# Pooled attention and a PReLU feed-forward on one core: PReLU from PSUM in the first chunk only, the first loads in runs, and a new order of the first phase

## The chip, the cores and the metric

The kernel runs on one core of one Trainium2 chip. A core has five engines that work side by side: TensorE (PE in the profile, with its weight loads as PEld), VectorE (DVE), ScalarE (ACT), GpSimd (POOL) and SyncE (SP), which here only issues DMAs. Each engine works through its own list of instructions in order and waits at semaphores for the others. PE writes into PSUM, a small memory of banks that DVE and ACT read; everything else lies in SBUF. The metric is the device time of one execution in microseconds (us); lower is better.

## The reference

```python
def _attn_ref(q, k, v):                      # each 8 x 8 x 576 x 64, f32
    k_p = k.reshape(B, H, Sp, pool, D).mean(axis=3)      # pool = 8, Sp = 72
    v_p = v.reshape(B, H, Sp, pool, D).mean(axis=3)
    scores = scale * np.matmul(q, k_p.transpose(0, 1, 3, 2))
    scores = scores - np.max(scores, axis=-1, keepdims=True)
    attn = np.exp(scores)
    attn = attn / (np.sum(attn, axis=-1, keepdims=True) + 1e-09)
    return np.matmul(attn, v_p)

def _moe_ref(x, w_in, w_out, alpha):         # x: 4608 x 512, the attention's output
    h = x @ w_in                             # w_in: 512 x 2048
    g = np.maximum(h, 0.0) + alpha * np.minimum(h, 0.0)
    return g @ w_out                         # w_out: 2048 x 512
```

The two weight matrices arrive as 64-bit floats, the rest as 32-bit ones.

## The kernel before

The 4608 tokens are worked on in 9 chunks of 512. PE multiplies 16-bit floats only, so every operand is scaled by a power of two and split into a high and a low half, and each product is three matmuls (low x high, high x low, high x high).

**One chunk.** Attention: k and v are pooled over 8 rows, q and k are split, `scores` (L598 to L600) makes the 128 x 576 scores of one of the four tiles of a chunk, and the softmax takes one of two paths. On the DVE path, DVE takes the maximum (L511), subtracts it (L525), ACT takes the exponential (L528), DVE sums (L530). On the ACT path, ACT does exponential and sum at once, head by head, in eight pairs of instructions (L521). Then the quotient (L536, POOL or DVE), the split into high half (ACT, L541, twice: the high half is needed at two places of the padded tile) and low half (POOL, L544 and L547), a transposing DMA (L552) and `mix` (L609), attention times v. ACT and DVE turn that into x (L566, L570). Feed-forward: for each of 16 slices f of 128 hidden units, "F1(f)" is twelve matmuls into one PSUM bank h (L766 to L768). ACT reads h and scales it to t in SBUF (`ffn1_scaled`, L772); DVE computes the larger of h x `ra` and t (`ffn1_prelu`, L776), reading h from PSUM; ACT rounds the result to the high half of g (L784), POOL subtracts for the low half (L787). F1(f) uses one of two h banks in turn, so F1(f+2) can start only when all readers of F1(f)'s bank are done. "F2" is 192 matmuls (L813 to L815) that sum g times the second weights into o; ACT scales o (L803) and SP stores it (L808).

**Two parts of the program.** The first phase (`start`) does the attention and feed-forward of chunk 0, loads and converts all weights, and does the attention of chunk 1. Its order is written by a planner (`_Plan`): each operation has an engine, an assumed duration, and a rank; the table `RK` holds the numbers that set the ranks and choose engines. The planner sets the order of every engine's list; the waits follow from what is read and written. A weight tile (two slices f) goes through: maximum over the high words (L242), scale factors, ACT on the low words (L647), ACT on the high words (L653 for the first weights, L657 for the second), two DVE operations that join the words (L660, L663), and for the first weights the high half on ACT (L683) and the low half on POOL (L702), for the second weights high on ACT (L688), low on DVE (L691). In chunk 0, FFN2 runs slice by slice over four banks, so its step f needs the second weights of slice f. `reduce_max` spreads a maximum over all partitions by ACT (L206), PE (L209) and DVE (L212, L217, then L233 and L238 for scale factors).

The other part is the loop over chunks 1 to 8: F1 and F2 of chunk c with the attention of chunk c+1 between them. Tile's scheduler sets its order. SP takes its list in order there too: the transposes of a chunk, then the k, q and v loads of the next but one, output stores, v loads.

Of the kernel before, what the change touches and what calls it, by code (L numbers as in the profile page):

```python
# [13 lines left out]
ALU = mybir.AluOpType  # L14
# [6 lines left out]
SP = S // POOL  # L21
# [3 lines left out]
P = 128  # L25
# [30 lines left out]
def _new_b(c):  # L56
# [2 lines left out]

RK = dict(k_pool=1, ps1=6, ps2=8, s_pool=0, w2_dve=16, lo_dve=0, l1=405.5, step=2.27, l2=548.61, mx1=198.3,
          mx1s=-26.1, mx2=186.66, mx2s=49.92, grp=52.93, grps=11.45, cv1=100.17, cv1s=47.71, r2=-639.49,
          cv2=443.89, cv2s=136.71, low1=145.54, low2=-143.62, lo1=644.52, lo2=79.0, sc=128.8, pre=-280.21,
          hi=98.27, lo=349.48, step2=33.01, a1=-147.09, al=314.3, td=99.45, ld1=42.46, ld2=-86.65, q0=186.92,
          v0=69.06, sm0=38.36, sms0=24.77, mix0=351.57, q1=94.05, v1=145.47, sm1=23.77, sms1=-49.07,
          mix1=-28.53)


ROOM = dict(d=3, big=12, f=4, e=3, v=3)  # L70
# [66 lines left out]
def pooled_attention_prelu_ffn(ctx: ExitStack, tc: tile.TileContext, qT, kT, vT, kN, vN, w1, w2, alpha, out):  # L137
# [56 lines left out]
    def reduce_max(add, r, m, n, *after, narrow=False, cap=None, rank=0.0):  # L194

        ps = once(lambda: ps_s.tile([P, 2, CH], F32, tag="s", name="pm"))
        t = once(lambda: sml.tile([P, n], F32, tag="pt", name="pt", bufs=2))

        def spread(j, dg):
            nc.scalar.activation(dg(), ident, AF.Copy, scale=m()[:, j:j + 1])  # L206
# [13 lines left out]
        xs_ = []  # L220
        for j in range(n):
            dg = once(lambda: sml.tile([P, P], BF16, tag="pd", name="pd", bufs=ROOM["d"]))
            x = add("ACT", 0.28, lambda j=j, dg=dg: spread(j, dg), *after, rank=rank, take="d")
            xs_.append(add("PE", 0.15, lambda j=j, dg=dg: bring(j, dg), x, rank=rank, take=None if j else "S", give="d"))
        return add("DVE", 0.4 + 0.13 * n, lambda: (maxima(), clamp()), *xs_, rank=rank, give="S")

# [26 lines left out]
    def load(add, dst, src, us, rank, *after, **kw):  # L253
        return add("SP", us, lambda: nc.sync.dma_start(out=dst(), in_=src), *after, rank=rank, **kw)  # L254
# [11 lines left out]
    def pooled(add, src, dst, rank, by_rows, behind=()):  # L266

        t = big_tile([P, 4, DM], "nat")  # L270
        u = once(lambda: fp.tile([P, DM], F32, tag="f", name="nat4"))
        ps = once(lambda: ps_s.tile([P, 2, CH], F32, tag="s", name="pl"))
        lds = []
        for j in range(2):
            lds += 2 * [load(add, lambda j=j: t()[:, 2 * j:2 * j + 2],
                             src[2 * j * P:(2 * j + 2) * P].rearrange("(a p) n -> p a n", p=P), 1.6, rank,
                             *behind, *lds[-1:], take=None if j else "big")]
        lds.append(load(add, lambda: u()[:S - 4 * P], src[4 * P:], 0.4, rank, lds[-1], take="f"))

        def products(j):  # L280
            rows, n = (t()[:, j], P) if j < 4 else (u(), S - 4 * P)
            win = pool[:n, w0 - P // POOL * j:w0 - P // POOL * j + SP]
# [18 lines left out]
    def big_tile(shape, name):  # L301
        return once(lambda: big.tile(shape, F32, tag="big", name=name))

    def attention(add, c, bs, rank, begin=False, early=False, k_pool=0, q_cuts=1, on_act=(), on_dve=(), behind=()):

# [27 lines left out]
        ql = []  # L333
        qt = big_tile([P, 2, NPR, HC], "qraw")
        for i in range(2):
            dst, dep = lambda i=i: qt()[:, i], [*behind, *[x[1] for x in ql]]
            if early and i == 0:
                dst, dep = lambda: kq()[:, NPR * S:].rearrange("p (a t) -> p a t", a=NPR), [kl[bs[0]][0][3]]
            ql.append((dst, load(add, dst, qT[c, i], 1.46, rank + 1, *dep, take="big" if i == early else None)))
# [159 lines left out]
        for i in range(TPC):  # L499
# [9 lines left out]
            def top(i=i, mx=mx, sv=sv):  # L509
                descale(c, i)  # L510
                nc.vector.tensor_reduce(out=mx(), in_=sv(), axis=AX.X, op=ALU.max)  # L511
            x = add("DVE", 0.8, top, x, rank=rk)
            nb = once(lambda: sml.tile([P, 2, 4], F32, tag="nb", name="nb", bufs=4))
            if i in on_act:
                x = add("DVE", 0.2, lambda i=i, nb=nb, mx=mx: nc.vector.tensor_scalar(
# [2 lines left out]
                for q in range(4):  # L518
                    def exps(i=i, ex=ex, nb=nb, sm=sm, sv=sv, b=q // 2, q=q % 2):
                        for h in (2 * q, 2 * q + 1):  # L520
                            nc.scalar.activation(ex()[:, b, h], sv()[:, b, h], AF.Exp, scale=descale(c, i),  # L521
                                                 bias=nb()[:, b, h:h + 1], accum_out=sm()[:, b, h:h + 1])
                    x = add("ACT", 0.8, exps, x, rank=rk, take=None if q else "e", give="S" if q == 3 else None)
            else:
                x = add("DVE", 0.73, lambda ex=ex, mx=mx, sv=sv: nc.vector.tensor_tensor(  # L525
                    out=ex(), in0=sv(), in1=mx().broadcast_to([P, 2, 4, SP]), op=ALU.subtract),
# [11 lines left out]
            ev_ = lambda ex=ex: ex().rearrange("p b h s -> p (b h) s")  # L538
            y = []
            for l in range(2):  # L540
                x = add("ACT", 0.67, lambda l=l, ap=ap, ev_=ev_: nc.scalar.copy(out=ap[:, l, :, :SP], in_=ev_()),  # L541
                        x, *td[i - 2:i - 1], rank=rk)
                y.append(x)
# [86 lines left out]
    def max_w(l, i):  # L630
        absmax((m1, m2)[l - 1][:, 2 * i:2 * i + 2], word(l, i, 1))

    def picked(f, n, of=NF):

        return (f + 1) * n // of > f * n // of

    def convert(add, l, i, begin, sc, rank):
# [8 lines left out]
        if wide:  # L646
            low = add("ACT", 1.15, lambda: nc.scalar.activation(  # L647
                word(l, i, 0).bitcast(I32), word(l, i, 0).bitcast(U32), AF.Copy, scale=LOW3), w_ld[l, i],
                      rank=rank + RK[f"low{l}"])
        if l == 1:  # L650
            x = begin
            for j in range(2):
                x = add("ACT", 0.66, lambda j=j: nc.scalar.activation(  # L653
                    u()[:, j], word(l, i, 1)[:, j], AF.Copy, scale=y1[:, 2 * i + j:2 * i + j + 1]),
                    begin, x, rank=rank, take=None if j else kind)
# [116 lines left out]
        nc.scalar.activation(t, hps[c, f], AF.Copy, scale=rp[:, f:f + 1])  # L772

    def ffn1_prelu(c, f):
        t = hs[c, f]
        nc.vector.scalar_tensor_tensor(out=t, in0=hps.pop((c, f)), scalar=ra[:, f:f + 1], in1=t,  # L776
                                       op0=ALU.mult, op1=ALU.max)

    def ffn1_parts(c, f, l):
# [46 lines left out]
    def start():  # L826
# [68 lines left out]
    class _Line:  # L895
# [5 lines left out]
        def add(self, engine, us, emit, *after, **kw):  # L901
            self.ops.append(emit)
# [59 lines left out]
```

## Time and profile before

| what | value |
|---|---|
| three runs | 907.07, 900.93, 902.24 us |
| median | 902.24 us |
| the profiled execution | 903.4 us, of which its span is 901.7 us |
| DVE, ACT, POOL busy | 407.2, 430.6, 347.8 us |
| bytes moved | HBM read 45.10 MB, written 9.44 MB |

The profile is of one execution. Its span is the time from the first to the last instruction; 1.7 us of the execution lie outside it. A row of the timeline has the start, the duration, the engine, the line, the tile written and those read, and in brackets how long the engine stood idle before it and what ended that. The table by stretches has, for each stretch, the busy time of each engine and PEclk, the share of full speed that TensorE's clock was granted. Times of the tables count from the start of the span.

### The profile page before, as it was taken

Reading aid. Unit: us, or ns where it says so; the run is one execution under the profiler, and the core shown is the slowest. Engines: PE = TensorE matmul, PEld = TensorE weight load, DVE = VectorE, ACT = ScalarE, POOL = GpSimd, SP = SyncE. Lnnn points to the kernel's source line nnn. Section 1 sums busy time; section 2 is a strip of 40 time slices with the busy share of each in tenths; the row PEclk is TensorE's granted clock in tenths of the full one; section 3 lists DMA queues with packets and bytes.
Section 4 is the critical chain, followed back from the end, with each engine's and each line's share of the span. In section 5 each row is a group of like instructions: output and inputs, shape, how many; then the busy total and the mean of one; then the engine's idle time right before and its main releaser. Section 6 shows DMA issues by size and latency. Waiting matters only on the chain.

```text
span 901.7 us, 11443 instructions
## 1 busy us (share of the span) xinstructions
PE 846.9 (94%) x4404; PEld 405.8 (45%) x4404; DVE 407.2 (45%) x657; ACT 430.6 (48%) x727; POOL 347.8 (39%) x375
## 2 busy tenths in 40 slices
PE   5779899989898989999989999999989999999998
PEld 4444354444344444454435444544444444444443
DVE  4889895484128520762077116621572145111110
ACT  5899984555324631563246234632464346313330
POOL 1357364376214730564055504640455027302320
PEclk9889999999999999999999999999999999999999
DMA  9686033606210360045012601260115004000000
GB/s 331 218 264 257 25 86 65 198 4 156 87 51 4 71 172 24 27 74 172 24 27 51 172 36 39 48 175 36 39 27 117 36 13 77 18 35 12 1 23 25
DMA packets 93638, 74.73 MB, mean 83 GB/s; under 512 B 77040, under 2 KB 77616, under 8 KB 93584
## 3 DMA queue, kind: packets, MB, share of 16 engines
q1 hardware_dynamic: 93584, 74.01, 29.2%
q8 instruction: 34, 0.56, 0.3%
q14 instruction: 20, 0.16, 0.1%
HBM read 45.10 MB, written 9.44 MB: 60 GB/s over the span
## 4 chain that ended last, share of the span: by engine, by line
PE 65%; DVE 11%; issue 7%; ACT 6%; DMA 6%; POOL 4%; SPq 1%; POOLq 0%; DVEq 0%; ACTq 0%
PE o L813 10%; PE o L814 10%; PE o L815 10%; PE h L766 9%; PE h L767 9%; PE h L768 9%; DMA vraw<-vT_dram 3%; POOL g L787 3%; DVE t L776 2%; DVE e L233 2%; DVE q L446 1%; PE x L609 1%; DMA nat<-kN_dram 1%; SPq L254 1%; ACT q L442 1%
## 5 line engine op out<-in xcount | busy, mean ns | idle before, releaser
L787 POOL TENSOR_TENSOR g<-t,g 128x512 f16<-128x512 f32 x144 | 166.9, 1160 | 397.7 <-ACT g L784 393.4
L776 DVE SCALAR_TENSOR_TENSOR t<-h,m,t 128x512 f32<-128x512 f32 x144 | 107.0, 744 | 308.4 <-ACT t L772 303.7
L766 PE MATMUL h<-x,w 128*128 128x512 f16 x576 | 220.0, 384 | 17.2 <-DVE t L776 13.9
L767 PE MATMUL h<-x,w 128*128 128x512 f16 x576 | 221.2, 384 | 0.0
L768 PE MATMUL h<-x,w 128*128 128x512 f16 x576 | 221.1, 384 | 0.0
L813 PE MATMUL o<-w,g 128*128 128x512 f16 x544 | 206.1, 380 | 10.7 <-POOL g L787 10.5
L814 PE MATMUL o<-w,g 128*128 128x512 f16 x544 | 206.4, 379 | 0.0
L815 PE MATMUL o<-w,g 128*128 128x512 f16 x544 | 204.4, 380 | 0.0
L772 ACT ACTIVATE t<-h,rp 128x512 f32<-128x512 f32 x144 | 97.5, 682 | 117.4 <-PE h L768 96.2
L784 ACT CAST g<-t 128x512 f16<-128x512 f32 x144 | 88.6, 615 | 99.0 <-DVE t L776 98.3
L803 ACT ACTIVATE o<-o,os 128x512 f32<-128x512 f32 x34 | 23.1, 687 | 156.3 <-PE o L815 156.3
L767 PEld LDWEIGHTS <-w 128*128 128x128 f16 x576 | 56.9, 99 | 83.4 <-issue 23.9
L813 PEld LDWEIGHTS <-g 128*128 128x128 f16 x576 | 56.3, 98 | 79.7 <-POOL g L787 13.1
L768 PEld LDWEIGHTS <-w 128*128 128x128 f16 x576 | 57.0, 99 | 69.7 <-issue 3.5
L815 PEld LDWEIGHTS <-g 128*128 128x128 f16 x576 | 56.4, 98 | 67.8 <-issue 0.3
L766 PEld LDWEIGHTS <-w 128*128 128x128 f16 x576 | 56.5, 99 | 65.9 <-issue 4.0
L814 PEld LDWEIGHTS <-g 128*128 128x128 f16 x576 | 56.4, 98 | 65.0 <-issue 0.6
L467 POOL TENSOR_TENSOR vraw<-vraw 72x512 f32<-72x512 f32 (+1 forms) x56 | 53.7, 972 | 43.0 <-DMA vraw<-vT_dram 39.2
L570 DVE SCALAR_TENSOR_TENSOR x<-x,xsc,x 128x512 f16<-128x512 f32 x36 | 26.1, 748 | 65.5 <-ACT x L566 65.5
L536 POOL TENSOR_TENSOR e<-e,sm 128x576 f32<-128x576 f32 x35 | 40.5, 1158 | 34.6 <-DVE sm L534 33.6
L541 ACT CAST apad<-e 128x576 f16<-128x576 f32 x72 | 44.9, 669 | 14.6 <-POOL e L536 12.4
L544 POOL TENSOR_TENSOR apad<-e,apad 128x448 f16<-128x448 f32 x36 | 37.3, 1035 | 17.7 <-ACT apad L541 17.6
(135 smaller groups left out, 840.6 us busy)
## 6 DMA issues: line engine op xcount, KB each, us to landing
w<-w_dram SPq DMA_DIRECT2D x16, 1024.0 KB
out_dram<-o SPq DMA_DIRECT2D x36, 256.0 KB
qraw<-qT_dram SPq DMA_DIRECT2D x17, 512.0 KB
vraw<-vT_dram SPq DMA_DIRECT2D x28, 288.0 KB
kraw<-kT_dram SPq DMA_DIRECT2D x12, 576.0 KB
kq<-kT_dram SPq DMA_DIRECT2D x2, 576.0 KB
nat<-kN_dram SPq DMA_DIRECT2D x2, 512.0 KB
nat<-vN_dram SPq DMA_DIRECT2D x2, 512.0 KB
```

Source lines behind the costliest of these rows:

```text
L467: nc.gpsimd.tensor_tensor(out=o, in0=y, in1=z, op=ALU.add)
L541: x = add("ACT", 0.67, lambda l=l, ap=ap, ev_=ev_: nc.scalar.copy(out=ap[:, l, :, :SP], in_=ev_()), x, *td[i - 2:i - 1], rank=rk)
L766: nc.tensor.matmul(ps, w[:, 1, ks_], x[:, 0], start=(n == 0), stop=False)
L767: nc.tensor.matmul(ps, w[:, 0, ks_], x[:, 1], start=False, stop=False)
L768: nc.tensor.matmul(ps, w[:, 0, ks_], x[:, 0], start=False, stop=(n == NK - 1))
L772: nc.scalar.activation(t, hps[c, f], AF.Copy, scale=rp[:, f:f + 1])
L776: nc.vector.scalar_tensor_tensor(out=t, in0=hps.pop((c, f)), scalar=ra[:, f:f + 1], in1=t, op0=ALU.mult, op1=ALU.max)
L784: nc.scalar.copy(out=g[:, 0], in_=t)
L787: nc.gpsimd.tensor_tensor(out=g[:, 1], in0=t, in1=g[:, 0], op=ALU.subtract)
L813: nc.tensor.matmul(ps, g[:, 1, ts_], w[:, 0], start=(f == 0), stop=False)
L814: nc.tensor.matmul(ps, g[:, 0, ts_], w[:, 1], start=False, stop=False)
L815: nc.tensor.matmul(ps, g[:, 0, ts_], w[:, 0], start=False, stop=(f == NF - 1))
```

## The change

Four things are changed.

1. `ffn1_prelu`: in chunks 1 to 8 DVE reads t instead of h, with `al` instead of `ra` (t is h times `rp`, and `ra` is `rp` times `al`, so it is the same quantity). Both inputs then lie in SBUF, and ACT is the only reader of the h bank. Chunk 0 is as before.
2. `pooled` and `attention`: the two halves of k (and of v) for chunk 0 are issued one behind the other as one operation of the planner; the q halves no longer count as dependent on each other.
3. The softmax paths are chosen by bits of `RK`: in chunk 0 only tile 2 takes the ACT path (tiles 0 and 2 before), in chunk 1 only tile 1 (tiles 0 and 1 before). The quotient of tile 0 goes from DVE to POOL. For tiles 0, 1 and 3 of chunk 0 the second copy of the high half is a DMA within SBUF instead of ACT.
4. A new table `RK` and some new assumed durations: a new order of the first phase. One of eight first-weight tiles has its low half on DVE instead of POOL, one of 16 second-weight slices on ACT and POOL instead of DVE, and one of eight second-weight tiles is joined in SBUF instead of PSUM.

Cut to its core:

```diff
-RK = dict(k_pool=1, ps1=6, ps2=8, s_pool=0, w2_dve=16, lo_dve=0, l1=405.5, step=2.27, l2=548.61, ...
+RK = dict(oa0=4, od0=0, oa1=2, ad0=11, ad1=0, v_pool=0, k_pool=1, ps1=6, ps2=7, s_pool=0, w2_dve=15, lo_dve=1,
...
-            lds += 2 * [load(add, lambda j=j: t()[:, 2 * j:2 * j + 2],
-                             src[2 * j * P:(2 * j + 2) * P].rearrange("(a p) n -> p a n", p=P), 1.6, rank,
-                             *behind, *lds[-1:], take=None if j else "big")]
+        def halves():
+            for j in range(2):
+                nc.sync.dma_start(out=t()[:, 2 * j:2 * j + 2],
+                                  in_=src[2 * j * P:(2 * j + 2) * P].rearrange("(a p) n -> p a n", p=P))
+        lds = 4 * [add("SP", 3.2, halves, *behind, rank=rank, take="big")]
...
+                if l and i in by_dma:
+                    y.append(add("SP", 0.5, lambda ap=ap: nc.sync.dma_start(out=ap[:, 1, :, :SP], in_=ap[:, 0, :, :SP]),
+                                 x, rank=rk))
+                    continue
...
     def ffn1_prelu(c, f):
-        t = hs[c, f]
-        nc.vector.scalar_tensor_tensor(out=t, in0=hps.pop((c, f)), scalar=ra[:, f:f + 1], in1=t,
+        t, h = hs[c, f], hps.pop((c, f))
+        nc.vector.scalar_tensor_tensor(out=t, in0=t if c else h, scalar=(al if c else ra)[:, f:f + 1], in1=t,
                                        op0=ALU.mult, op1=ALU.max)
...
-        xd, td = attention(add, 0, [0], 0.0, begin=True, q_cuts=2, on_act=(0, 2), on_dve=(0,))
+        xd, td = attention(add, 0, [0], 0.0, begin=True, q_cuts=2, on_act=bits("oa0"),
+                           on_dve=bits("od0"), by_dma=bits("ad0"))
```

Three places of the order. First SP's list from the start: `nat` is k or v of chunk 0 (by its `kN` or `vN` source), `qraw` is q, `al` is alpha, `w` a weight tile. Before:

```order
L254 DMA nat<-kN_dram 128x2x512
L254 DMA qraw<-qT_dram 128x1024
L254 DMA al<-al_dram 128x16
L254 DMA w_134<-w_dram 128x2x1024
L254 DMA nat<-kN_dram 128x2x512
L254 DMA qraw<-qT_dram 128x1024
L254 DMA w_175<-w_dram 128x2x1024
L254 DMA nat_193<-kN_dram 64x512
```

Now:

```order
L276 DMA nat<-kN_dram 128x2x512 x2
L254 DMA nat_132<-kN_dram 64x512
L254 DMA qraw<-qT_dram 128x1024 x2
L254 DMA al<-al_dram 128x16
L254 DMA w_163<-w_dram 128x2x1024
L254 DMA w_180<-w_dram 128x2x1024
L276 DMA nat<-vN_dram 128x2x512 x2
L254 DMA nat_243<-vN_dram 64x512
```

All of k, then all of q, stand ahead of the first weight tile, and v stands behind the second weight tile instead of behind the eighth.

Second, DVE's list in the first phase around the last PReLUs of chunk 0 (`t`): `w_605` and `w_681` are the first second-weight slices (L691, now L705, is their low half), `kbd` and `q` the low halves of chunk 1's k and q. Before:

```order
L429 SCALAR_TENSOR_TENSOR kbd_95<-ks,s,kbd_95 64x4x72
L691 SCALAR_TENSOR_TENSOR w_605<-v,s_124,w_605 128x512
L429 SCALAR_TENSOR_TENSOR kbd_95<-ks,s,kbd_95 64x4x72
L446 SCALAR_TENSOR_TENSOR q_982<-kq,s,q_982 128x1024
L663 SCALAR_TENSOR_TENSOR v<-w_703,vw 128x1024
L776 SCALAR_TENSOR_TENSOR t<-h,m_122,t 128x512 x2
L585 TENSOR_SCALAR ds<-e 128x1
```

Now:

```order
L790 SCALAR_TENSOR_TENSOR t<-h,m_122,t 128x512
L432 SCALAR_TENSOR_TENSOR kbd_95<-ks,s,kbd_95 64x4x72
L705 SCALAR_TENSOR_TENSOR w_681<-v,s_124,w_681 128x512
L432 SCALAR_TENSOR_TENSOR kbd_95<-ks,s,kbd_95 64x4x72
L449 SCALAR_TENSOR_TENSOR q_1032<-kq,s,q_1032 128x1024
L705 SCALAR_TENSOR_TENSOR w_681<-v,s_124,w_681 128x512
L677 SCALAR_TENSOR_TENSOR v<-w_754,vw 128x1024
```

The low halves of k, q and of the first second-weight slices have moved from ahead of the last PReLU to behind it.

Third, PE's list behind the mix for chunk 2 (the row with `aT` and `v16`), with the semaphores it waits for. Before:

```order
L609 MATMUL x_2263<-aT_1908,v16_1836 64x384
L766 LDWEIGHTS w1_134 [waits DVE_49]
L766 MATMUL h_2390<-x16_2257,w1_134 128x512 [waits Activation_49]
L766 LDWEIGHTS w1_134
L766 MATMUL h_2422<-x16_2257,w1_134 128x512 [waits DVE_49]
L813 LDWEIGHTS g_2128 [waits Pool_49]
L813 MATMUL o_2131<-w2_784,g_2128 128x512
```

Now, and (the last row) further down at the third F1 of that chunk:

```order
L616 MATMUL x_2289<-aT_1934,v16_1862 64x384
L827 LDWEIGHTS g_1669
L827 MATMUL o_2312<-w2_681,g_1669 128x512
```

```order
L780 MATMUL h_2482<-x16_2283,w1_163 128x512 [waits Activation_49]
```

Before, two products of the next chunk's F1 and an F2 product that reads the chunk's last slice of g stand directly behind the mix; now F2 of the chunk's third tile, with the oldest slice of g, stands there. An F1 that takes over an h bank waited for DVE and now waits for ACT.

More of the change, by code (lines that the diff above doesn't have):

```diff
@@ L58, in _new_b @@
     return [b for _, _, b in _segs(c) if b > prev]
[L62 to L67, printed above, removed]
+RK = dict(oa0=4, od0=0, oa1=2, ad0=11, ad1=0, v_pool=0, k_pool=1, ps1=6, ps2=7, s_pool=0, w2_dve=15, lo_dve=1,
+          l1=451.63, step=2.76, l2=439.38, mx1=223.95, mx1s=-38.27, mx2=267.52, mx2s=50.59, grp=66.84,
+          grps=8.65, cv1=-42.31, cv1s=60.37, r2=-403.82, cv2=826.06, cv2s=147.64, low1=83.05, low2=-213.14,
+          lo1=717.27, lo2=97.15, sc=136.57, pre=-255.44, hi=44.61, lo=345.22, step2=29.56, a1=-20.76,
+          al=308.29, td=-23.43, ld1=94.39, ld2=42.23, q0=321.84, v0=94.52, sm0=-105.72, sms0=0.87, mix0=310.16,
+          q1=66.1, v1=144.72, sm1=133.56, sms1=-54.48, mix1=58.45)
 ROOM = dict(d=3, big=12, f=4, e=3, v=3)
@@ L222, in reduce_max @@
             dg = once(lambda: sml.tile([P, P], BF16, tag="pd", name="pd", bufs=ROOM["d"]))
-            x = add("ACT", 0.28, lambda j=j, dg=dg: spread(j, dg), *after, rank=rank, take="d")
+            x = add("ACT", 0.39, lambda j=j, dg=dg: spread(j, dg), *after, rank=rank, take="d")
             xs_.append(add("PE", 0.15, lambda j=j, dg=dg: bring(j, dg), x, rank=rank, take=None if j else "S", give="d"))
@@ L272, in pooled @@
         ps = once(lambda: ps_s.tile([P, 2, CH], F32, tag="s", name="pl"))
-        lds = []
-        for j in range(2):
-            lds += 2 * [load(add, lambda j=j: t()[:, 2 * j:2 * j + 2],
-                             src[2 * j * P:(2 * j + 2) * P].rearrange("(a p) n -> p a n", p=P), 1.6, rank,
-                             *behind, *lds[-1:], take=None if j else "big")]
-        lds.append(load(add, lambda: u()[:S - 4 * P], src[4 * P:], 0.4, rank, lds[-1], take="f"))
+        def halves():
[3 more added lines that the diff above has]
+        lds = 4 * [add("SP", 3.2, halves, *behind, rank=rank, take="big")]
+        lds.append(load(add, lambda: u()[:S - 4 * P], src[4 * P:], 0.4, rank, take="f"))
         def products(j):
@@ L302, in big_tile, with attention @@
         return once(lambda: big.tile(shape, F32, tag="big", name=name))
-    def attention(add, c, bs, rank, begin=False, early=False, k_pool=0, q_cuts=1, on_act=(), on_dve=(), behind=()):
+    def attention(add, c, bs, rank, begin=False, early=False, k_pool=0, q_cuts=1, on_act=(), on_dve=(), by_dma=(),
+                  behind=()):
         n = len(bs) + 2
@@ L335, in attention @@
         for i in range(2):
-            dst, dep = lambda i=i: qt()[:, i], [*behind, *[x[1] for x in ql]]
+            dst, dep = lambda i=i: qt()[:, i], [*behind, *([] if begin else [x[1] for x in ql])]
             if early and i == 0:
@@ L511, in top @@
                 nc.vector.tensor_reduce(out=mx(), in_=sv(), axis=AX.X, op=ALU.max)
-            x = add("DVE", 0.8, top, x, rank=rk)
+            x = add("DVE", 0.95, top, x, rank=rk)
             nb = once(lambda: sml.tile([P, 2, 4], F32, tag="nb", name="nb", bufs=4))
@@ L522, in exps @@
                                                  bias=nb()[:, b, h:h + 1], accum_out=sm()[:, b, h:h + 1])
-                    x = add("ACT", 0.8, exps, x, rank=rk, take=None if q else "e", give="S" if q == 3 else None)
+                    x = add("ACT", 1.25, exps, x, rank=rk, take=None if q else "e", give="S" if q == 3 else None)
             else:
@@ L631, in max_w, with bits @@
         absmax((m1, m2)[l - 1][:, 2 * i:2 * i + 2], word(l, i, 1))
+    def bits(name):
+        return [i for i in range(TPC) if RK[name] >> i & 1]
     def picked(f, n, of=NF):
@@ L649, in convert @@
                       rank=rank + RK[f"low{l}"])
-        if l == 1:
+        if l == 1 and picked(i, RK["v_pool"], NF // 2):
+            x = add("Pool", 2.3, lambda: nc.gpsimd.tensor_tensor(
+                out=u(), in0=word(l, i, 1), in1=y1[:, 2 * i:2 * i + 2].broadcast_to([P, 2, 512]), op=ALU.mult),
+                begin, rank=rank, take=kind)
+        elif l == 1:
             x = begin
             for j in range(2):
-                x = add("ACT", 0.66, lambda j=j: nc.scalar.activation(
+                x = add("ACT", 0.72, lambda j=j: nc.scalar.activation(
                     u()[:, j], word(l, i, 1)[:, j], AF.Copy, scale=y1[:, 2 * i + j:2 * i + j + 1]),
@@ L887, in start @@
             x = [add("PE", 2.59, lambda f=f: step(f), gd[f], wd[2, f], *x, rank=due[2](f))]
-        attention(add, 1, [1], L2 + RK["a1"], early=True, k_pool=int(RK["k_pool"]), on_act=(0, 1), behind=[ld[2, NF // 2 - 1]])
+        attention(add, 1, [1], L2 + RK["a1"], early=True, k_pool=int(RK["k_pool"]), on_act=bits("oa1"),
+                  by_dma=bits("ad1"), behind=[ld[2, NF // 2 - 1]])
         for i in (2, 3, 0, 1):
```

## The prediction

> **What bounds the kernel now.** I read the page, the table by stretches, PE's waits, then the timeline where PE stood. The page:
>
> ```profile
> PE 846.9 (94%) x4404; PEld 405.8 (45%) x4404; DVE 407.2 (45%) x657; ACT 430.6 (48%) x727; POOL 347.8 (39%) x375
> ```
>
> PE is busy for 94% of the span of 901.7 us. What can be won without touching PE's own work is its 54.8 us of idle time and what a slow clock costs. Whose they are is told by cutting the span at the first F1 matmul (62.03), the end of chunk 0's F1 (111.6) and the first F1 of chunk 1 (161.7). The columns are length, then busy time of PE, PEld, DVE, ACT, POOL, then PEclk, DMA share and GB/s:
>
> ```profile
> 0.00:62.03 62.03, 40.88 (x246) 28.42 (x246) 42.94 (x95) 47.27 (x101) 20.24 (x34) 0.91 0.80 257
> 62.03:111.60 49.57, 45.87 (x198) 19.60 (x196) 46.84 (x65) 46.01 (x68) 29.97 (x24) 0.94 0.45 176
> 111.60:161.70 50.10, 47.48 (x285) 23.44 (x286) 38.51 (x61) 32.38 (x73) 25.32 (x31) 1.00 0.34 68
> 161.70:901.69 739.99, 712.63 (x3678) 334.35 (x3677) 278.95 (x438) 304.94 (x489) 272.23 (x287) 0.99 0.24 63
> ```
>
> Four stretches, four limits. The opening is ACT's and the loads'. In F1 of chunk 0 DVE (46.84) and ACT (46.01) are both full. F2 of chunk 0 is PE's. In chunks 1 to 8 PE is busy for 712.63 of 739.99, and 27.4 us are idle. PE's two long waits there (us in total, times, longest):
>
> ```profile
> PE h L766 <- DVE t L776: 12.9, 7, 2.6
> PE o L813 <- POOL g L787: 10.5, 6, 3.4
> ```
>
> So 12.9 us go to F1 waiting for DVE's PReLU to give the h bank back, and 10.5 us to F2 waiting for the low half of g. Two of these waits in the timeline; the first is in chunk 2:
>
> ```profile
> 273.46 1.15 POOL L787 TENSOR_TENSOR g<-t,g 128x512 f16<-128x512 f32 x1
> 273.53 2.79 DVE L233 TENSOR_SCALAR e<-pr 128x3 int32<-128x3 int32 x1
> 274.57 0.61 POOL L467 TENSOR_TENSOR vraw<-vraw 72x256 f32<-72x256 f32 x1
> 275.14 1.15 POOL L787 TENSOR_TENSOR g<-t,g 128x512 f16<-128x512 f32 x1
> 276.73 1.09 ACT L426 ACTIVATE kbd<-ks,s 64x288 f16<-64x288 f32 x2 [2.47 <-DVE s L238]
> 277.30 1.36 DVE L429 SCALAR_TENSOR_TENSOR kbd<-ks,s,kbd 64x288 f16<-64x288 f32 x2
> 277.85 2.19 ACT L442 ACTIVATE q<-qraw,s 128x1024 f16<-128x1024 f32 x2
> 279.03 2.48 DVE L446 SCALAR_TENSOR_TENSOR q<-qraw,s,q 128x1024 f16<-128x1024 f32 x2 [0.37 <-ACT q L442]
> 279.94 1.24 ACT L772 ACTIVATE t<-h,rp 128x512 f32<-128x512 f32 x2
> 281.43 0.75 DVE L776 SCALAR_TENSOR_TENSOR t<-h,m,t 128x512 f32<-128x512 f32 x1
> ...
> 282.23 0.38 PE L766 MATMUL h<-x,w 128*128 128x512 f16 x1 [2.32 <-DVE t L776]
> 282.44 0.38 PE L767 MATMUL h<-x,w 128*128 128x512 f16 x1
> ```
>
> A DVE instruction on three numbers takes 2.79 us, ending as three POOL instructions in a row end (276.29). ACT's k and q work waits behind it, ACT reaches t at 279.94, DVE the PReLU at 281.43, and PE starts at 282.23. Matmuls follow each other at 0.215 us. The second wait is at the seam of two chunks:
>
> ```profile
> 230.76 3.06 POOL L467 TENSOR_TENSOR vraw<-vraw 72x512 f32<-72x512 f32 x3 [7.03 <-DMA vraw<-vT_dram]
> 233.78 1.15 POOL L787 TENSOR_TENSOR g<-t,g 128x512 f16<-128x512 f32 x1
> 234.99 0.39 PE L813 MATMUL o<-w,g 128*128 128x512 f16 x1 [3.43 <-POOL g L787]
> ```
>
> POOL sat at v instructions whose load was late; g stood behind them and PE behind g.
>
> **The change, chunks 1 to 8.** The PReLU keeps its count and its size; read from SBUF I give it the 0.74 us it has now:
>
> ```profile
> L776 DVE SCALAR_TENSOR_TENSOR t<-h,m,t 128x512 f32<-128x512 f32 x144 | 107.0, 744 | 308.4 <-ACT t L772 303.7
> L691 DVE SCALAR_TENSOR_TENSOR w<-v,s,w 128x512 f16<-128x512 f32 x16 | 13.5, 880 | 0.0
> L784 ACT CAST g<-t 128x512 f16<-128x512 f32 x144 | 88.6, 615 | 99.0 <-DVE t L776 98.3
> ```
>
> L691 is the same operation with both inputs in SBUF and takes 0.88. What changes is who frees the bank: the order shows PE waiting for ACT. At 282 that would have been about 280.6 (first t of the pair at 279.94, 0.69 long) instead of 282.2, so 1.5 of that 2.3 us. The new PE order does more. Counted from the built order at 0.215 us a matmul, between the last F1 product of a slice and the first F2 that reads its g there were 3.8 to 5.3 us of other PE work at the start of chunks 1 to 8, now 7.9 in chunks 2 to 8 (5.6 in chunk 1); between F1(0) and F1(2) 1.2 to 2.7, now 2.7 (0.4 in chunk 1). A slice needs t, PReLU and high half (0.68 + 0.74 + 0.62) and POOL's 1.16, 3.2 us in all with no queue, so 7.9 leaves room for the 3.4 us wait above. And the seam is gone: half of the mixes no longer have an F2 on the newest g behind them.
>
> Against it stands that DVE's 128 PReLUs now may meet POOL. Here is one that did, in the opening:
>
> ```profile
> 26.29 0.73 DVE L446 SCALAR_TENSOR_TENSOR q<-qraw,s,q 128x512 f16<-128x512 f32 x1
> 27.13 2.46 POOL L702 TENSOR_TENSOR w<-v,w 128x1024 f16<-128x1024 f32 x1 [8.94 <-ACT w L683]
> 27.61 2.52 DVE L446 SCALAR_TENSOR_TENSOR q<-qraw,s,q 128x512 f16<-128x512 f32 x1
> ```
>
> The same operation takes 0.73, and 2.52 when it comes while POOL works: it ends 0.54 us after POOL does. The Trainium skill says so in general ("SBUF — State Buffer", section "Who interferes with whom"): a DVE instruction with two SBUF inputs contends with a GpSimd instruction that reads SBUF, and whoever comes second is blocked for the other's whole length. The trace agrees, with 2.52 against 0.73. POOL is busy for 272.23 of 740 us, and one g takes 1.16, so a PReLU that arrives at random waits 0.37 x 0.58 = 0.2 us, and 1.16 behind a full one. Both are less than the new room, so I count the price as nothing on the path; its upper bound is the first rival.
>
> So of 27.4 us idle I keep 8 (chunk 1's short distances, the k and q work on ACT, which still holds t) and take back 2 of the some 7 us that PEclk 0.99 costs: 712.6 - 2 + 8 = 719, that is -21. Bounds: no idle and full clock 707; nothing won 740.
>
> **The opening.** The chain of waits there runs along ACT for most of its last 18 us. The rows that price this part and the next (the first from the chain, the second from stretches of 36 us, the third again from the chain):
>
> ```profile
> 32.94 3.26 ACT e L521 x16
> 0.00:36.00 36.00, 21.89 (x142) 18.26 (x142) 22.67 (x53) 23.36 (x48) 6.65 (x16) 0.98 0.90 329
> 198.09 1.75 DMA v<-v
> L528 ACT ACTIVATE e<-e,ds 128x576 f32<-128x576 f32 x32 | 24.8, 774 | 10.6 <-DVE e L525 10.3
> L541 ACT CAST apad<-e 128x576 f16<-128x576 f32 x72 | 44.9, 669 | 14.6 <-POOL e L536 12.4
> L647 ACT ACTIVATE w<-w 128x1024 int32<-128x1024 uint32 x16 | 18.1, 1149 | 2.8 <-DMA w<-w_dram 2.8
> L653 ACT ACTIVATE vw<-w,y 128x512 f32<-128x512 f32 x12 | 8.7, 722 | 0.6 <-DVE x L570 0.5
> L683 ACT CAST w<-v 128x1024 f16<-128x1024 f32 x8 | 8.3, 1036 | 0.1
> L663 DVE SCALAR_TENSOR_TENSOR v<-w,vw 128x1024 int32<-128x1024 int32 x14 | 17.1, 1219 | 0.0
> 113.64 1.40 DVE L776 SCALAR_TENSOR_TENSOR t<-h,m,t 128x512 f32<-128x512 f32 x2
> 145.60 2.28 DVE L691 SCALAR_TENSOR_TENSOR w<-v,s,w 128x512 f16<-128x512 f32 x3
> ```
>
> Ahead of its first t, ACT has eight exponential pairs fewer (3.26 us), three copies (2.0), two L653 (1.4) and one L683 (1.0), and one more L528 (0.8): -6.9 us. But DVE now sets a bound. The loads are the same 11.8 MB (36 us at 329 GB/s), so the last weight tile still lands at about 35; k and v only come sooner. After the maximum of that tile, DVE has, counted from the order at the rows' durations, about 18 us of work until the first x: 35 + 18 + 3 for waits = 56, and F1 at 57 instead of 62. That is -5; bounds 0 (DVE's waits are 8) and -6.9. No row shows the copies by DMA that replace ACT's; the nearest, a copy of v within SBUF, takes 1.75 us, and tile 3's stands straight ahead of the last transpose: 1.75 for 0.67, which the 3 us hold. If they cost nothing that way, ACT is the bound and F1 starts at 55.1.
>
> **F1 of chunk 0.** Between first and last t, ACT loses two q (2.2), two k (1.1) and two low words (2.3), and gains two L653 (1.4), one L683 (1.0) and a high half (0.6): -2.6. DVE loses four L691 (3.5), one q (1.2) and two k (1.4), and gains two operations as long as a join (2.4): -3.7. Both full engines shrink, ACT less, so 49.6 becomes 47.0; bounds 41.3 (192 matmuls) and 49.6.
>
> **F2 of chunk 0.** What left F1 arrives here: three L691 (2.6), a q (1.2), two k (1.4), one more join (1.2), and subtraction and sum of a tile on the DVE path (some 1.5), so DVE's 38.5 becomes 46.4 of 50.1. PE covers that only while each second-weight slice is ready for its FFN2 step. Before, the last L691 ended at 147.88, 32.8 us after the last PReLU at 115.04, with 26.7 us of work by the order, 1.23 times as long. The new order puts slice 13 at 32.5 us of work, x 1.23 = 40; PReLU ends some 2 us after F1, so 42 after F1's end, where PE comes at 37.5. So a wait of some 4.5 us against the 2.6 idle now: 52.0, +1.9. Bounds 47.5 and 57.
>
> **Sum** against the profiled execution: 57 + 47 + 52 + 719 = 875 span, +1.7 outside = 876.7 against 903.4. The median lies 1.2 lower, so 875.5.
>
> **Rivals.**
> - *Lock-out.* POOL's instructions follow each other without a gap, and the row at 273.53 shows DVE losing three times running. In the interleaved part a slice takes PE 18 x 0.215 = 3.9 us, and ACT's list alternates t and high half, so t of the next slice waits for the PReLU: 0.68 + 0.74 + 0.62 = 2.0. It decides from a mean wait of 1.9 us per PReLU. At two full g (2.3) each of 13 slices in 8 chunks loses 0.4: +42, with the old idle time kept and 7 won before: 937. Against it: POOL's g needs the PReLU itself, so POOL runs dry. 6%. If whoever comes second is always blocked, as that page has it, this is where it shows.
> - *The idle time stays.* ACT's k and q work (3.3 us from 276.73) still stands ahead of t, and the 2.79 us wait still comes. Then 719 is 738: 894. 16%.
> - *The first phase gives nothing.* DVE sets the start and then FFN2: 62 + 49.6 + 55 + 719: 886. 18%.
> - *The bank isn't freed sooner.* The order's wait on ACT excludes it; with what else could fail, 4% at 902.
>
> **How the numbers follow.** The forecast has 56% and its own range 864 to 886. The range of 8 in 10 takes in the third rival and nearly the second: 861 to 893. A measurement of this kernel can tell about 1% (9 us) from no change: faster 0.83, same 0.11, slower 0.06.
>
> **What would show it.** F1 starts at 55 to 59. In chunks 1 to 8 "PE h <- DVE t" is gone and "PE o <- POOL g" is under 4 us; PE's idle time there is 3 to 14. L790 has a mean between 0.75 and 1.1; over 2.5 is the first rival. Chunk 0's FFN2 shows PE waiting for DVE's second-weight halves. I am wrong if PE waits for ACT t by more than 12 us in the chunks, or if F1 starts after 60.

## The result and the profile after

The changed kernel takes 878.12 us (median of 874.56, 877.46, 878.79 and 878.85) against 902.62 us: a ratio of 0.971, with an interval of 0.967 to 0.976. The forecast was 875.5. The sum is nearly right, but its parts are not. The profiled execution has a span of 877.1 us; the page's line of engines, and the stretches cut at the same places as before (first F1, end of chunk 0's F1, first F1 of chunk 1):

```profile
PE 840.6 (96%) x4445; PEld 406.5 (46%) x4445; DVE 429.4 (49%) x658; ACT 422.8 (48%) x695; POOL 371.1 (42%) x376
```

```profile
0.00:66.95 66.95, 45.36 (x286) 31.05 (x287) 40.35 (x92) 40.16 (x79) 19.31 (x34) 0.80 0.76 228
66.95:115.50 48.55, 43.46 (x199) 18.95 (x198) 47.48 (x60) 45.14 (x68) 32.44 (x25) 1.00 0.52 203
115.50:165.09 49.59, 48.03 (x285) 23.50 (x283) 39.97 (x65) 33.67 (x60) 24.48 (x31) 1.00 0.34 79
165.09:877.05 711.96, 703.79 (x3680) 332.96 (x3678) 301.59 (x442) 303.86 (x491) 294.82 (x287) 1.00 0.24 65
```

| stage | before | forecast | after |
|---|---|---|---|
| opening, to the first F1 | 62.0 | 57.0 | 67.0 |
| F1 of chunk 0 | 49.6 | 47.0 | 48.5 |
| F2 of chunk 0 | 50.1 | 52.0 | 49.6 |
| chunks 1 to 8 | 740.0 | 719 | 712.0 |

The chunks won 28.0 us instead of 21, and the opening lost 4.9 us where it was to win 5. The misses nearly cancel: the opening is 10.0 us over the forecast and F1 1.5, the chunks are 7.0 under it and F2 2.4. That the sum came out is luck. One of the prediction's own signs of being wrong came true, too: F1 starts after 60.

**The chunks.** PE stands for 8.2 us there (711.96 - 703.79) instead of 27.4. Of both, 3.8 us lie behind the last matmul. PE's longest waits in that stretch, then DVE's PReLU on the page and by its line (there the durations in ns are shortest, median, longest):

```profile
PE o L827 <- POOL g L801: 2.9, 3, 1.1
PE h L781 <- DVE x L577: 0.7, 1, 0.7
PE h L780 <- ACT t L786: 0.6, 2, 0.4
```

```profile
L790 DVE SCALAR_TENSOR_TENSOR t<-t,al 128x512 f32<-128x512 f32 x128 | 123.8, 969 | 267.6 <-ACT t L786 253.0
```

```profile
L790 DVE SCALAR_TENSOR_TENSOR t<-t,al x128: 732/752/2609, 175.4 to 846.6; 128x512 f32<-128x512 f32 x128
```

The wait for DVE's PReLU (12.9 us before) is gone, the wait for POOL's g fell from 10.5 to 2.9. The median PReLU is as long as before, the longest 2.6 us, and the mean 0.969. So DVE does wait for POOL, and nothing of it reaches PE.

**The opening.** PE's timeline from tile 3's scores on, with the rows of the single scores left out, then DVE's rows that had a wait ahead of them:

```profile
37.03 0.28 PE L605 MATMUL s<-kbd,q 128*128 128x144 f16 x1 [7.97 <-ACT e L524]
...
38.42 10.47 PE L849 MATMUL idle<-pool 128*128 128x256 f16 x74
48.73 0.28 PE L209 MATMUL pm<-pd,ones 128*128 128x128 bf16 x2
...
65.08 1.94 PE L616 MATMUL x<-aT,v 88*64 88x512 f16 x16 [1.27 <-DVE v L677]
66.95 0.39 PE L780 MATMUL h<-x,w 128*128 128x512 f16 x1
```

```profile
38.66 0.76 DVE L514 TENSOR_REDUCE mx<-s 128x8 f32<-128x576 f32 x1 [6.93 <-PE s L607]
...
48.99 0.29 DVE L212 TENSOR_REDUCE pt<-pm 128x1 f32<-128x128 f32 x1 [2.32 <-PE pm L209]
...
59.70 1.23 DVE L674 SCALAR_TENSOR_TENSOR vw<-vw,w 128x1024 int32<-128x1024 int32 x1 [0.83 <-ACT vw L667]
...
67.48 1.41 DVE L577 SCALAR_TENSOR_TENSOR x<-x,xsc,x 128x512 f16<-128x512 f32 x2 [2.83 <-ACT x L573]
```

The scores of tile 3 wait 8 us for a PSUM bank. Behind them stand 74 idle matmuls, which the planner puts where it expects PE to stand, and behind these the products (L209) that spread the maxima of v and of the first weights. DVE stands first for the scores, then for those products. While PE stands, its granted clock falls to 0.50, so the idle matmuls that follow are slow as well; two stretches of 4 us:

```profile
32.00:36.00 4.00, 0.00 (x0) 0.00 (x0) 0.00 (x0) 4.00 (x15) 3.79 (x5) 0.50 0.45 153
36.00:40.00 4.00, 2.97 (x20) 2.50 (x20) 1.34 (x2) 0.98 (x6) 0.91 (x2) 0.50 0.80 141
```

Why the bank was late is in PE's list. `reduce_max` takes room for its PSUM tile with the first of its products, but the other products don't wait for the first. In the new order the last three of the first group of four (`pm_328`) stand ahead of tile 2's scores, and the first stands behind the idle matmuls (the rows of the built order with the buffers' numbers, without weight loads):

```
L209 MATMUL pm_328<-pd_324,ones_105 128x128 [waits Activation_49]
L209 MATMUL pm_328<-pd_326,ones_105 128x128 [waits Activation_49]
L209 MATMUL pm_328<-pd_330,ones_105 128x128 [waits Activation_49]
...
L605 MATMUL s_356<-kbd0_94,q16_176 128x144 [waits Activation_49]
...
L849 MATMUL idle_420<-pool_111 128x256
...
L209 MATMUL pm_495<-pd_374,ones_105 128x128 [waits PE_49]
L209 MATMUL pm_328<-pd_320,ones_105 128x128
```

So they hold one of the two bank pairs from 27.4 us until DVE has read them at 51.4, and tiles 2 and 3 share the other one.

The products `pl` that pool k and v in the opening are of 32-bit floats, so "PE multiplies 16-bit floats only" holds for the other products alone.

### The profile page after: what moved, and what is told of

It reads as the page before. It is cut to its first block, busy times and chain, and to the rows that moved or that the text cites. A ratio compares the mean times of both kernels' runs of the same rounds, so it can differ in the third digit from the quotient of the medians.

```text
span 877.1 us, 11487 instructions
## 1 busy us (share of the span) xinstructions
PE 840.6 (96%) x4445; PEld 406.5 (46%) x4445; DVE 429.4 (49%) x658; ACT 422.8 (48%) x695; POOL 371.1 (42%) x376
## 4 chain that ended last, share of the span: by engine, by line
PE 83%; DVE 8%; ACT 3%; DMA 3%; issue 1%; SPq 1%; ACTq 0%
PE o L827 13%; PE o L828 13%; PE o L829 13%; PE h L780 12%; PE h L781 12%; PE h L782 12%; PE x L616 2%; DVE m L242 1%; DMA nat<-vN_dram 1%; DVE v L677 1%; DMA qraw<-qT_dram 1%; PE idle L849 1%; DVE t L790 1%; PE s L605 1%; PE s L606 1%
## 5 line engine op out<-in xcount | busy, mean ns | idle before, releaser
L801 POOL TENSOR_TENSOR g<-t,g 128x512 f16<-128x512 f32 x144 | 174.5, 1214 | 345.5 <-ACT g L798 342.9
L790 DVE SCALAR_TENSOR_TENSOR t<-t,al 128x512 f32<-128x512 f32 x128 | 123.8, 969 | 267.6 <-ACT t L786 253.0
L780 PE MATMUL h<-x,w 128*128 128x512 f16 x576 | 218.2, 379 | 3.7 <-DVE t L790 2.1
L781 PE MATMUL h<-x,w 128*128 128x512 f16 x576 | 218.3, 379 | 2.7 <-DVE x L577 2.7
L782 PE MATMUL h<-x,w 128*128 128x512 f16 x576 | 218.3, 379 | 0.0
L470 POOL TENSOR_TENSOR vraw<-vraw 72x512 f32<-72x512 f32 (+1 forms) x56 | 56.8, 1031 | 54.7 <-DMA vraw<-vT_dram 50.8
L539 POOL TENSOR_TENSOR e<-e,sm 128x576 f32<-128x576 f32 x36 | 45.5, 1269 | 56.6 <-DVE sm L537 44.5
L548 ACT CAST apad<-e 128x576 f16<-128x576 f32 x69 | 43.0, 668 | 24.9 <-POOL e L539 17.8
L551 POOL TENSOR_TENSOR apad<-e,apad 128x448 f16<-128x448 f32 x36 | 39.5, 1096 | 4.0 <-ACT apad L548 3.9
```

The source lines that it names most:

```text
L470: nc.gpsimd.tensor_tensor(out=o, in0=y, in1=z, op=ALU.add)
L539: x = add("DVE" if i in on_dve else "Pool", us, lambda ex=ex, sm=sm, eng=eng: eng.tensor_tensor(out=ex(), in0=ex(), in1=sm().broadcast_to( ...
L780: nc.tensor.matmul(ps, w[:, 1, ks_], x[:, 0], start=(n == 0), stop=False)
L781: nc.tensor.matmul(ps, w[:, 0, ks_], x[:, 1], start=False, stop=False)
L782: nc.tensor.matmul(ps, w[:, 0, ks_], x[:, 0], start=False, stop=(n == NK - 1))
L790: nc.vector.scalar_tensor_tensor(out=t, in0=t if c else h, scalar=(al if c else ra)[:, f:f + 1], in1=t, op0=ALU.mult, op1=ALU.max)
```

## The experiments

All stages are of the profiled execution, in us; the ratios are to the kernel before on the same chip. Kernels with added lines have line numbers that are one to four higher in their profiles.

| kernel | opening | F1 | F2 | chunks | median | ratio (95%) |
|---|---|---|---|---|---|---|
| before | 62.0 | 49.5 | 50.1 | 740.0 | 902.6 | |
| the change | 67.0 | 48.5 | 49.6 | 712.0 | 878.1 | 0.971 (0.967 to 0.976) |
| prelu_alone | 61.9 | 49.9 | 50.1 | 708.3 | 873.2 | 0.967 (0.963 to 0.971) |
| rest_alone | 66.5 | 47.9 | 49.7 | 739.9 | 907.6 | 1.006 (1.004 to 1.009) |
| hold_bank | 66.6 | 48.0 | 49.5 | 756.8 | 926.5 | 1.025 (1.021 to 1.029) |
| short_fill | 62.8 | 48.5 | 49.6 | 713.5 | 875.5 | 0.969 (0.966 to 0.972) |
| own_bank | 59.2 | 48.7 | 49.6 | 713.2 | 871.3 | 0.965 (0.962 to 0.968) |
| own_bank_short | 57.3 | 48.8 | 49.8 | 711.7 | 869.5 | 0.963 (0.960 to 0.966) |
| old_order_bank | 62.4 | 48.8 | 50.1 | 708.1 | 871.3 | 0.965 (0.961 to 0.968) |
| all_but_numbers | 59.0 | 46.1 | 60.7 | 712.2 | 880.5 | 0.975 (0.971 to 0.979) |
| prelu_twice | 66.6 | 48.5 | 49.5 | 745.0 | 911.3 | 1.008 (1.005 to 1.011) |
| prelu_thrice | 66.6 | 47.8 | 49.8 | 807.9 | 974.0 | 1.079 (1.075 to 1.083) |
| one_input | 64.7 | 48.7 | 50.0 | 721.0 | 885.8 | 0.982 (0.980 to 0.984) |

**The two parts of the change by themselves.** The first is the kernel before with the new `ffn1_prelu`, the second the changed kernel with the old one.

> The kernel before with only the PReLU edit (chunks 1 to 8 read t). Theory: the two parts of the change add up. The first phase stays at before's 161.7 us to the first F1 of chunk 1, the chunks take after's 712.0 us instead of 740.0, so with 1.7 us outside the span 875 us, within 2: about 27 faster than before and some 3 faster than the whole change. PE's waits for the PReLU in the chunks are gone and its clock there is full. Rival: the chunks are short only because the new first phase hands over another state (or the full clock was luck of one execution): then half of the gain or less, 886 to 895.

> The changed kernel with the PReLU reading PSUM in all chunks, so the first phase of after with the chunks of before. Theory: 165.1 + 740.0 + 1.7 = 907 us, within 3, so 3 to 5 slower than before: the new first phase costs instead of winning. F1 of chunk 0 starts at 67. Rival: the new first phase wins in the chunks what it loses in the opening: 890 to 902.

Both theories hold. The PReLU edit alone gives 873.2 us (875 expected), all else alone 907.6 (907 expected). The whole gain is the PReLU's; the new first phase costs 4 to 5 us. prelu_alone has the PE order of the change in the chunks from chunk 2 on, and rest_alone very nearly the old one, with its old waits (14.8 us for DVE's PReLU, 8.8 for POOL's g).

**Is it the bank, or the place of the inputs?**

```diff
+        if c:
+            nc.vector.scalar_tensor_tensor(out=held, in0=h[:, :1], scalar=1.0, in1=t[:, :1],
+                                           op0=ALU.mult, op1=ALU.max)
```

> The changed kernel with one more DVE instruction per slice in chunks 1 to 8, behind the PReLU, that reads one column of h: the PReLU still reads SBUF, but the bank is given back by DVE again, as before. Theory (the gain is the earlier release of the bank and the PE order that follows from it): the gain is lost, 905 to 915 us, and PE waits for DVE at F1 again, 10 us or more. Rival (the gain is that the PReLU's inputs lie in SBUF, or that the clock is full): 878 to 884, since 128 small instructions of some 0.1 to 0.2 us hide.

```profile
PE o L831 <- POOL g L805: 17.2, 9, 6.8
PE h L781 <- DVE held L794: 13.7, 7, 2.2
```

The PReLU reads SBUF as in the change, but DVE gives the bank back, and the gain is gone: 926.5, worse than the 905 to 915 expected. The PE order is again close to the old one, with single slices between (12 F1 products, some 6 F2 products). The 128 small instructions take 0.153 us each, 19.6 in all, against a loss of 48 us on the change; 128 instructions of 0.68 us that don't hold the bank cost 7.7 us (one_input, below), so the loss isn't that of the instructions as such. The rival is excluded: reading SBUF wins nothing by itself. The earlier release and the order that follows from it can't be told apart here, since the scheduler makes the one from the other.

**The opening: idle matmuls and bank.** The first kernel keeps 12 of the 74 idle matmuls (the expectation's words in brackets on how many are left out are wrong; the number ahead of them holds). The second changes no engine's list, only the bank that `pm` lies in:

```diff
-            for _ in range(n):
+            for _ in range(12 if n == 74 else n):
```

```diff
-        ps = once(lambda: ps_s.tile([P, 2, CH], F32, tag="s", name="pm"))
+        ps = once(lambda: ps_o.tile([P, DM], F32, tag="o", name="pm").rearrange("p (b n) -> p b n", b=1)
+                  if narrow and n == 4 else ps_s.tile([P, 2, CH], F32, tag="s", name="pm"))
```

> The changed kernel with 12 instead of 74 idle matmuls behind the scores of tile 3 (they compute nothing; one is left out of every six or so), all else in the same order. Theory: those 10.3 us of idle matmuls stand ahead of the maxima of v and of the first weights on PE, so the maxima come when ACT's spread is done, at 45.8 instead of 49.0, and F1 of chunk 0 starts 3 us earlier, at 64: 875 us. Rival 1: DVE's own 22.9 us of work between tile 3's maximum and the first x sets the start: 877 to 878. Rival 2: with fewer matmuls the granted clock stays at half and what is won is lost again: 878 to 882.

> The changed kernel, every engine's list the same, but the maxima of the two groups of four first-weight slices are gathered in a PSUM bank of the output's pool, which is unused then, instead of one of the two bank pairs that the scores use. Theory (three of the four products of the first group fill a pair at 27.4 and the fourth stands behind the 74 idle matmuls, so the pair is held from 27.4 to 51.4 and tiles 2 and 3 share the other): tile 3's scores start at 29 instead of 37, PE's 8.0 us wait is gone, the idle matmuls end at 40 instead of 48.9, and F1 of chunk 0 starts at 60 to 63: 871 to 874 us. Rival 1: weights' loads and DVE's own work set the start, F1 at 66, 877 us. Rival 2: it is ACT's late exponentials of tile 2, and the scores wait anyway: 878 us.

> The changed kernel with the own bank for the maxima and 12 instead of 74 idle matmuls behind the scores of tile 3. Theory: bank and idle matmuls are one chain, in which whichever is later counts, so both together win less than the sum: F1 of chunk 0 at 59 to 62, 869 to 873 us. Rival: the two gains add up (4 from the matmuls, 4 to 7 from the bank): F1 at 56 to 58, 866 to 868 us. Second rival: DVE's work then is the limit and it is as with the short fill alone, 875 us.

The three medians came as the theories had them: 875.5, 871.3 and 869.5 us. F1 started earlier than they had it: at 62.8 instead of 64, at 59.2 instead of 60 to 63, and at 57.3 instead of 59 to 62. The last lies where the rival of own_bank_short had it, but the gains don't add up: 4.2 and 7.8 us by themselves, 9.7 together. PE's rows of own_bank, and the stretch from 35 us to the first F1 of own_bank_short:

```profile
28.98 8.24 PE L850 MATMUL idle<-pool 128*128 128x256 f16 x74
37.06 0.28 PE L210 MATMUL pm<-pd,ones 128*128 128x128 bf16 x2
...
59.19 0.39 PE L781 MATMUL h<-x,w 128*128 128x512 f16 x1
```

```profile
35.00:57.30 22.30, 12.31 (x87) 8.51 (x86) 19.90 (x38) 16.00 (x31) 12.04 (x16) 0.69 0.72 142
```

With its own bank the 8 us wait is gone, the idle matmuls start at 28.98 instead of 38.42 and take 8.24 instead of 10.47, since the clock is at full speed there. With both edits F1 starts at 57.3, where the prediction had it (57), and DVE works for 19.90 of the last 22.30 us: now it is the limit that the prediction counted. own_bank_short has the lowest median of this study, below the kernel before and below the change.

**Does the old order have the same faults?** The kernel before with the new `ffn1_prelu`, the same bank, and at most 12 idle matmuls at each place.

> The kernel before with the PReLU edit, and with the two edits that mended the opening of the changed kernel: the maxima of the groups of four gathered in the output's pool, and at most 12 idle matmuls at each place (50, 25 and 29 before). Theory (the new order is worth about the 5 us that were forecast, and lost them to the bank and the idle matmuls alone): the old order gains little from them, F1 of chunk 0 at 59.5 to 62, 870 to 873 us, so slower than the changed kernel with both edits (869.5). Rival (the old order had the same two faults): F1 at 57 and 867 us or less, and the new order is worth nothing.

It gains nothing in the opening (62.4 against 61.9 in prelu_alone; the theory had 59.5 to 62). Its second mix starts 0.4 us sooner (60.57 against 60.95) and takes 1.92 us instead of 1.06, since with fewer idle matmuls the clock is at half there; so the bank holds up little in the old order, and the faults are the new order's own. Without them the new order is worth 62.4 - 57.3 = 5.1 us there, or 4.6 against prelu_alone. By medians no gain is shown: 869.5 against 871.3, with ratios whose intervals overlap. Chunk 1 of the new order is longer, 93.1 us from F1 to F1 against 89.1, which makes it 711.7 against 708.1 in the chunks.

**What the numbers of the table do.** The changed kernel with before's numbers in `RK`, but the new paths and loads.

> The changed kernel with before's numbers for the ranks in the table (loads in runs, softmax paths and copies by DMA as changed; the second weights' low halves and joins on the engines of before), so another order of the first phase. Theory (the paths and loads take 5 to 7 us from ACT ahead of F1, the order only has to let it through): F1 of chunk 0 at 58 to 66, 870 to 878 us. Rival (the numbers are what makes the order usable): over 880 us.

```profile
105.12:165.78 60.66, 50.50 (x290) 23.96 (x287) 45.20 (x71) 34.83 (x63) 23.07 (x30) 0.92 0.26 56
```

```profile
PE o L828 <- DVE w L705: 10.0, 2, 7.5
```

F1 starts at 59.0, so with before's numbers the paths and loads make the opening 3.0 us shorter. But 880.5 us is outside the theory's range and just inside the rival's: F2 of chunk 0 takes 60.7 us and PE waits 10.0 us for DVE's second-weight halves. That is the wait that the prediction feared of the change; the new numbers avoid it.

**How much room has the PReLU?** One or two more instructions of the PReLU's form go ahead of it in chunks 1 to 8; in one_input it is a maximum over t instead, as long but with a single input in SBUF. No result of these is used.

```diff
+        if c:
+            extra = wp.tile([P, CH], F32, tag="v", name="extra", bufs=ROOM["v"])
+            nc.vector.scalar_tensor_tensor(out=extra, in0=t, scalar=al[:, f:f + 1], in1=t, op0=ALU.mult, op1=ALU.max)
```

> The changed kernel with a second DVE instruction of the PReLU's size and inputs in front of each of the 128 PReLUs of chunks 1 to 8, whose result is not used. It puts 0.75 to 1 us more between t and g of every slice. Theory (the new order leaves 7.9 us from a slice's F1 to its F2 and 3.9 us from slice to slice in the interleaved part, of which ACT's t, the PReLU and the high half need 2.3): it hides, 878 to 884 us. Rival (the PReLU is at the limit already, since DVE loses against POOL): 0.5 us or more on each of 13 slices in 8 chunks, over 925 us.

> As with the PReLU twice, but two more DVE instructions in front of each PReLU, 1.5 to 2 us more per slice, which is where the prediction's first rival was to decide (a mean wait of 1.9 us). Theory: t, DVE's three and the high half come to 3.9 to 4.3 us for a slice, as long as PE's 3.9, so it starts to cost: 885 to 915 us. Rival (t of the next slice doesn't wait for the PReLU, so DVE alone would have to be full): within 5 us of the PReLU twice.

Both miss: 911.3 where 878 to 884 was expected, and 974.0 where it was 885 to 915. One place in chunk 2 of prelu_twice, by DVE, POOL, ACT and PE:

```profile
314.38 1.37 DVE L792 SCALAR_TENSOR_TENSOR extra<-t,al 128x512 f32<-128x512 f32 x1
315.79 1.53 DVE L793 SCALAR_TENSOR_TENSOR t<-t,al 128x512 f32<-128x512 f32 x1
```

```profile
314.05 1.15 POOL L539 TENSOR_TENSOR e<-e,sm 128x576 f32<-128x576 f32 x1
315.16 1.60 POOL L804 TENSOR_TENSOR g<-t,g 128x512 f16<-128x512 f32 x1
```

```profile
317.35 0.62 ACT L801 CAST g<-t 128x512 f16<-128x512 f32 x1 [0.87 <-DVE t L793]
317.87 0.68 ACT L786 ACTIVATE t<-h,rp 128x512 f32<-128x512 f32 x1
```

```profile
318.61 0.38 PE L780 MATMUL h<-x,w 128*128 128x512 f16 x1 [0.96 <-ACT t L786]
```

DVE's two instructions take 2.9 us instead of 1.5, each ending 0.55 us after a POOL instruction (at 315.20 and 316.76), and POOL's g takes 1.60 instead of 1.15. ACT's high half waits for DVE, the next t stands behind it, and PE waits for t. That is the chain of the prediction's first rival, and it starts at one more instruction of 0.75 us, not at a mean wait of 1.9. To tell the lock-out from mere length:

> As with the PReLU twice (911 us), but the extra DVE instruction in front of each PReLU is a maximum over t: as long (about 0.7 us by the rows of the maxima), with a single input in SBUF, and PE's order is nearly that of the PReLU twice. The result is not used. Theory (what broke the PReLU twice is that two instructions with both inputs in SBUF wait for POOL and make POOL wait, 0.98 us instead of 0.74 and 1.26 instead of 1.16): the maximum is not stretched, 880 to 895 us. Rival (any 0.7 us more between t and g costs as much, since ACT's t of the next slice stands behind the high half): 903 to 911 us.

```profile
L793 DVE SCALAR_TENSOR_TENSOR t<-t,al 128x512 f32<-128x512 f32 x128 | 112.9, 884 | 7.1 <-DVE extra L242 0.5
L242 DVE TENSOR_REDUCE extra<-t 128x1 f32<-128x512 f32 x128 | 86.8, 680 | 225.2 <-ACT t L786 225.1
```

885.8 us, in the theory's range. 128 instructions of 0.68 us with one input cost 7.7 us, as many with two inputs, 0.75 long when nothing is in the way, cost 33.2 (in the chunks 9.0 and 33.0). So some 25 us of the 33 go with the lock-out: the two-input instruction waits for POOL (its mean is 0.993), and POOL for it. Two things were not held equal: the maximum writes one column instead of 512, and PE's order in the two kernels is close but not the same.

## Why the prediction was right or wrong

**Chunks: the mechanism right, the size too small.** The bank is freed by ACT, the waits for DVE and at the seams go, and 8.2 us of PE's idle time stay where 8 were kept. That the two agree is in part luck: in both kernels 3.8 us of the idle time lie behind the last matmul (before it ends at 897.92 of 901.69), which the prediction didn't set apart. Between matmuls PE stood for 23.6 us before and stands for 4.4 now. The term that was mis-sized is the clock: 2 us were taken back, and PE's busy time fell by 8.8 (712.63 to 703.79). Three stretches of before at half clock show where 5.1 of them were, at 1.7 each:

```profile
235.60:239.01 3.41, 3.41 (x9) 1.22 (x8) 0.43 (x1) 2.42 (x4) 0.00 (x0) 0.50 0.27 98
283.38:286.79 3.41, 3.41 (x13) 1.51 (x12) 0.27 (x2) 0.90 (x2) 1.87 (x3) 0.50 0.00 0
471.12:474.53 3.41, 3.41 (x10) 1.22 (x9) 0.45 (x1) 0.85 (x2) 2.24 (x2) 0.50 0.02 5
```

Two of them follow the two waits that the prediction quoted (ends at 234.99 and 282.23). A pause of 2.3 to 3.4 us costs itself and, now and then, 1.7 us of slow clock. With the pauses gone, no stretch of the chunks is at half clock until the last matmuls. Some 2 of the other 3.7 us are in the mix, whose matmuls are busy for 16.15 us before and 13.85 now; where the rest is stays open.

**PReLU against POOL: priced right, its margin wrong.** The mean wait was worked out as 0.2 us, and the mean rose from 0.744 to 0.969. That it costs nothing on the path holds (2.9 us of waits for g). The Trainium skill ("SBUF — State Buffer", section "Who interferes with whom") has whoever comes second wait for the other's whole length; here one PReLU sat out more than that, the end of one POOL instruction and the whole of the next. It ends at 449.53, 0.55 us behind the second (448.98), while a third already runs (the last row holds two):

```profile
446.92 2.61 DVE L790 SCALAR_TENSOR_TENSOR t<-t,al 128x512 f32<-128x512 f32 x1 [1.79 <-ACT t L786]
```

```profile
446.61 1.15 POOL L801 TENSOR_TENSOR g<-t,g 128x512 f16<-128x512 f32 x1
447.72 2.28 POOL L470 TENSOR_TENSOR vraw<-vraw 72x512 f32<-72x512 f32 x2
```

The same section says that a DVE instruction with at most one SBUF input doesn't contend, outside the modes in which it uses two ports; the maxima of one_input agree, at 0.63 to 0.69 us throughout. One input alone is not enough: the L233 of the prediction, 2.79 us long beside POOL, has one as well. But the bound "decides from a mean wait of 1.9 us" was wrong. It set 2.0 us for t, PReLU and high half against PE's 3.9 and left out that ACT and DVE do the next chunk's attention in the same slices: in prelu_twice, ACT has 2.0 us of it between the t at 312.34 and the one at 317.87.

**Opening: wrong.** The step that failed is "35 + 18 + 3 for waits = 56". The 18 us of DVE's work were about right, as own_bank_short shows (19.90). The 3 us for waits were not: DVE stood for about 10 of the 32.5 us from 35 to the first x in the change, because of what stood in PE's list. Another 2.6 us of its work were still to do at 35 (22.53 us, against 19.90 in own_bank_short), since it had stood from 31.7 on: 35 + 22.5 + 10 = 67.5. The prediction compared the lists of ACT and DVE there and took PE's as given; the order of the products, scores and idle matmuls on PE, and who holds the bank, weren't read. That the opening had no gain was the third rival's case, but its reason (DVE's work) isn't what the runs show.

**F1 of chunk 0: 48.5 instead of 47.0.** DVE was to shrink by 3.7 us and is busy for 47.48 against 46.84: a PReLU more falls into the stretch, and joins in SBUF are stretched (two L674 at a mean of 1.55 us).

**F2 of chunk 0: 49.6 instead of 52.0.** The wait for the second weights didn't come (0.2 us). Their slices 13 and 14 were done at 153.8, 36 us after the last PReLU (117.8), where 40 was worked out; the factor of 1.23 between counted and real time, taken from the kernel before, was 1.1 here. all_but_numbers shows that the fear was of the right thing.

## What to carry to other kernels

When two instructions on different engines read one buffer, the later reader sets when it comes free; letting the earlier engine be its only reader is worth the wait and what the scheduler then does with the room. Of a new order, read the list of every engine that hands out a shared bank, fillers too: an idle matmul in an in-order list is work to whatever stands behind it. And price a pause of TensorE with the slow clock that may follow it.

## What was not expected of the hardware

- The half clock comes in steps of 3.41 us and needs no pause of that length: in the chunks of before, pauses of 2.32 and 2.55 us were followed by one (as was one of 3.43), others of 2.42 and 2.29 us were not. The three steps start whole multiples of 3.413 us apart (at 235.60, 283.38 and 471.12). On that grid, the pauses of 2.32 and 2.55 us fell nearly whole into one step; those of 2.42 and 2.29 us lay across an edge, with at most 1.6 us in one step. The page "TensorE: Matmul & The Clock Gate" of the Trainium skill (section "Part 1: The HAM clock gate") has a window of 3413 ns that runs freely, and the clock at half after at least one idle window. The steps agree; that it takes a whole idle window doesn't, since these pauses are shorter than one.
- Two instructions with both inputs in SBUF, one after the other on DVE, cost about four times as much as one of them with a maximum of about the same length (33.2 against 7.7 us). POOL loses as well: its g has a mean of 1.258 us in prelu_twice, 1.214 in the change and 1.160 before.
